# Moving a quad's data in parts: bulk transfers by batch and transposed loads by half tiles in a chunked recurrence kernel

## The chip, the cores and the metric

The kernel runs on one core of a Trainium2 chip. The core has five engines with a queue each: TensorE (PE in the profile; its weight loads are PEld), VectorE (DVE), ScalarE (ACT), GpSimd (POOL) and SyncE (SP). Each runs its own instructions in order and waits on semaphores for the others. Nearly every data transfer of this kernel is issued by SP, one DMA instruction after another, and carried out by 16 DMA engines that all queues share. The metric is the time of one launch on the device in microseconds (us); the lower the better. The time before is the median of three runs.

## What is computed

A recurrence over 768 tokens for 4 batches x 8 heads with a 40 x 40 state per head, and then a layer of two matrix products with h cos(h) between them, over the 3072 tokens:

```python
for t in range(S):                     # S = 768; B, H, D = 4, 8, 40
    y[:, :, t] = einsum('bhd,bhde->bhe', r_t, state)
    Sa = einsum('bhde,bhe->bhd', state, a_t)
    state = state * w_t[:, :, None, :] - einsum('bhd,bhe->bhde', Sa, b_t)
    state = state + einsum('bhd,bhe->bhde', v_t, k_t)
x = y.transpose(0, 2, 1, 3).reshape(B * S, H * D)      # 3072 x 320
h = x @ w_in                                            # 320 x 2048
out = (h * cos(h)) @ w_out                              # 2048 x 320
```

## The kernel before

**Chunks.** The tokens are cut into 24 chunks `c` of 32 tokens, so that 4 batches x 32 tokens fill 128 partitions. Within a chunk the recurrence is turned into small matrix products: `p1` (four segments w, a, b, n) prepares w's products over the chunk and the matrix `nps` whose triangular inverse is needed; `p2` (v, k, g) turns v, k and r and makes the `gram` products; `main` (t, q, x, s, z) carries the state: `ch_t` turns the state (`sT`) and copies it to `s`, `ch_q` reads r, `ch_x` and `ch_s` solve, `ch_z` makes the new state in `qz` and the output `yt`. p1 runs about four chunks ahead, p2 one ahead.

**The layer.** `tokens(c)` stores `yt` to HBM (`xd`, L881) and reads it back as `xT` (L891, L893). For each pair `g` of chunks, 16 "pieces" follow: `first_a`/`first_b` multiply `xT` by w_in (`ph`), ACT and DVE take the cosine (`turns`, L935 to L945), and `second` multiplies by w_out (`po`). The pieces of pair g are allowed from chunk 2g + 2 on; they fill TensorE between the segments of the recurrence.

**The order.** It is written out by hand. For each chunk a list `segs` names segments and places `M` for pieces. `step(work)` runs one segment's Python, which appends its instructions to every engine's queue; then each entry of `waiting` is counted down by one, and what reaches zero is appended. `later(n, work)` puts work there: it stands in the queues n steps later. A step is a position in the queues, not a time.

**Quads.** From chunk 8 on, w, a and r are not turned by TensorE. They come by quads `q` of four chunks, with 32 heads (b, h) x 4 chunks on 128 partitions:

- `ws_fetch(q)` (L164) reads w for a quad into `ws`: one DMA of 128 rows of 5 KB. `ws_scan` makes running products W on DVE. `ws_store` (L247) writes `ws` to HBM (`wd`), from where `load` (L155) reads w in natural order.
- `quad_fetch` (L186) reads a or r into a tile `raw`, one DMA as well. `quad_a` makes a~ = a times the product before it, permuted to d before t (`flip`, L227 on DVE and L232 on ACT), in four slices of d, one a step. `quad_flip` permutes r or W in four copies on ACT (L213, 128 x 320 each).
- `quad_store` writes a `flip` to HBM as `td`: for a~ and W one DMA (L200), whose row order is that of the partitions; for r four (L203), one for each batch, as r's rows are ordered with the head outermost.
- `fetch_T` (L243) reads a chunk of `td` into a transposed tile, in two DMAs, one for each half of the partitions: W into `wb` and a~ into `aT` (`fetch_aw`), r into `rT` (`fetch_r`). `own_w` on POOL (L487, L466) then takes columns of `wb`; POOL's `ch_z` of that chunk reads them.
- `raw` and `flip` share the two buffers of the tag `cv`.

`scanned(q)` is a segment that stands near the end of chunks 4, 8, 12 (for q = 3, 4, 5), within chunk 3 (q = 2), and in the start (q = 1). It scans quad q's w and then schedules, in steps from there: wd's store at 2, a~'s four slices at 1 to 4 and its store at 6, r's fetch (quad q - 1) at 7, its copies at 12 to 15 and its store at 17, W's copies at 18 to 21 and its store at 23, the next quad's w at 25 and a at 26. r of the last quad has a place of its own in chunk 17: fetch at 1, copies at 6 to 9, store at 11.

`p1_w(c)` for c from 8 issues the loads of two chunks of W at once (four DMAs), `p1_a(c)` later those of a~ (four DMAs). `p1_b` calls `own_w` for both chunks at once. `query` issues `fetch_r(c + 2)` one step after `ch_q(c)`.

Of the kernel before, what the change touches and what calls it, by code (L numbers as in the profile page):

```python
# [9 lines left out]
F32 = mybir.dt.float32  # L10
# [10 lines left out]
def kernel(  # L21
# [43 lines left out]
    nc = tc.nc  # L65
    B, H, S, D = r.shape
    P, C, DP = 128, 32, 64
    HH = H // 2
    NCH = S // C
# [89 lines left out]
    ws = const.tile([P, C, D], F32, tag="ws", name="ws")  # L159
    wd = {}  # L160

    def ws_fetch(q, via=nc.sync):
        n = 4 * C * D
        via.dma_start(  # L164
            ws.rearrange("p t d -> p (t d)"),
            bass.AP(w.tensor, w.offset + q * n, [[S * D, B * H], [C * D, 4], [1, C * D]]),
        )

    def ws_scan(q):
        n = 1  # L170
# [9 lines left out]

    td = {}

    def quad_fetch(n, q, via=nc.sync):
        raw = sb2.tile([P, C, D], F32, tag="cv", name="raw")
        x = src[n]
        via.dma_start(  # L186
            raw.rearrange("p t d -> p (t d)"),
            bass.AP(x.tensor, x.offset + q * 4 * C * D, [[S * D, B * H], [C * D, 4], [1, C * D]]),
        )
        G["raw", n] = raw  # L190

    def quad_tile():
        return sb2.tile([P, D, C], F32, tag="cv", name="flip")

    def quad_store(n, q, t, of_heads):
        to = dram.tile([4, H * B, D * C], F32, tag=f"td_{n}", name="td")
        td[n, q] = to
        x = t.rearrange("p d t -> p (d t)")
        if not of_heads:
            nc.sync.dma_start(to.rearrange("c m x -> m c x"), x)  # L200
            return
        for i in range(B):
            nc.sync.dma_start(to.rearrange("c (h b) x -> b h c x", b=B)[i], x[blk[i]])  # L203

    def quad_flip(n, q, raw, of_heads, start):

        t = []

        def part(i):
            if not i:  # L210
                t.append(quad_tile())
            ds = slice(i * D // 4, (i + 1) * D // 4)
            nc.scalar.copy(t[0][:, ds], raw()[:, :, ds].rearrange("p t d -> p d t"))  # L213

        for i in range(4):
            later(start + i, lambda i=i: part(i))
        later(start + 5, lambda: quad_store(n, q, t[0], of_heads))

    def quad_a(q, start):
        t = []  # L220

        def part(i):
            raw = G["raw", "a"]
            if not i:
                t.append(quad_tile())
            ds = slice(i * D // 4, (i + 1) * D // 4)
            nc.vector.tensor_tensor(  # L227
                t[0][:, ds, 1:], raw[:, 1:, ds].rearrange("p t d -> p d t"),
                ws[:, : C - 1, ds].rearrange("p t d -> p d t"), ALU.mult,
            )  # L230
            if i == 3:
                nc.scalar.copy(t[0][:, :, 0:1], raw[:, 0:1].rearrange("p t d -> p d t"))  # L232

        for i in range(4):
            later(start + i, lambda i=i: part(i))
        later(start + 5, lambda: quad_store("a", q, t[0], False))

    def fetch_T(n, c, dst, of_heads):

        x = td[n, c // 4][c % 4].rearrange("m (d t) -> d m t", t=C)  # L240
        for e in range(2):
            at_e = x[:, 4 * B * e : 4 * B * (e + 1)] if of_heads else x[:, e::2]
            nc.sync.dma_start(dst[half[e]].rearrange("p (m t) -> p m t", t=C), at_e)  # L243

    def ws_store(q):
        wd[q] = dram.tile([B, H, 4, C, D], F32, tag="wd", name="wd")
        nc.sync.dma_start(wd[q].rearrange("b h c t d -> (b h c) (t d)"), ws.rearrange("p t d -> p (t d)"))  # L247

    for c in range(2):
        load(c, "w", parts=range(2))  # L250
# [159 lines left out]
    def later(steps, work):  # L410
        waiting.append([steps, work])
# [17 lines left out]
    def p1_w(c):  # L429
        if c >= QT:  # L430
            if c == 8:
                later(2, lambda: over_w(c, unpad(nat["w", c])))
            else:
                over_w(c, unpad(nat["w", c]))
            for i in range(2):
                fetch_aw(c + i, "w")
            return
        ps = at("wT")
        for i in range(2):
            turned(ps[:, i], nat["w", c + i])  # L440
        if c < 4:

            for i in range(2):
                nc.scalar.copy(G["w1"][:, i, :, 0:1], b4(ps[:, i])[:, :, 0:1])
            nc.vector.memset(ps[:, :, ::C], 0.0)
        for i in range(2):
            wb = wb_b[(c + i) % 7]
            if c < 4:
                nc.vector.tensor_tensor_scan(
                    wb[:, 1:], ps[:, i], flat(G["w1"][:, i]), 0.0, ALU.mult, ALU.add  # L450
                )
            else:
                nc.scalar.copy(wb[:, 1:], ps[:, i])
            wc = ring.tile([P, 4 * B], F32, tag="wc", name="wc")
            nc.gpsimd.tensor_copy(wc, wb[:, C::C])
            G["wb", c + i] = wb
            G["wx", c + i] = wb[:, : 4 * P].rearrange("p (f m b t) -> p f m b t", f=2, m=2, t=C)
            G["wc", c + i] = wc.rearrange("p (f m b) -> p f m b", f=2, m=2)
            if c >= 4:
                from_one(c + i)  # L460
        if c >= 4:
            over_w(c, unpad(nat["w", c]))
# [8 lines left out]
        nc.gpsimd.tensor_tensor(unpad(bn_b[c % 7]), unpad(nat["b", c]), rw, ALU.mult)  # L471
        G["rw", c] = rw

    def fetch_aw(c, n):

        if n == "a":
            G["aT", c] = ring.tile([P, B, 4, C], F32, tag="aT", name="aT")
            fetch_T("a", c, G["aT", c].rearrange("p b j t -> p (b j t)"), False)
            return
        wb = wb_b[c % 7]  # L480
        fetch_T("w", c, wb[:, 1:], False)
        G["wb", c] = wb

    def own_w(c):
        wb = G["wb", c]
# [14 lines left out]
    def p1_a(c):  # L500
        if c >= QT:
            over_w(c + 1, unpad(nat["w", c + 1]))
            for i in range(2):
                fetch_aw(c + i, "a")
            return
        if c >= 4:
            ps = at("aps")
            for i in range(2):
                turned(ps[:, i], nat["a", c + i])
            for i in range(2):  # L510
                a_W(c + i, ps[:, i])
            over_w(c + 1, unpad(nat["w", c + 1]))
            return
        for c in range(c, c + 2):
            wn = ps_h.tile([P, 512], F32, tag="h", name="wn")
            aps = ps_o.tile([P, 512], F32, tag="o", name="aps")
            for j in range(4):
                nc.tensor.transpose(
                    wn[:, j * P : (j + 1) * P], G["wb", c][:, j * P + 1 : (j + 1) * P + 1], ident
                )  # L520
            from_one(c)
            turned(aps, nat["a", c])
            over_w(c, unpad(wn.rearrange("p (h d) -> p h d", h=H)))
            a_W(c, aps)

    def p1_b(c):
        ps = at("bT")
        for i in range(2):
            turned(ps[:, i], bn_b[(c + i) % 7])
        for i in range(2):  # L530
            bT = sb3.tile([P, 4, P], F32, tag="opT", name="bT")
            nc.scalar.copy(bT.rearrange("p j t -> p (j t)"), ps[:, i])
            G["bT", c + i] = bT
            if c >= QT:
                own_w(c + i)
        if c == 2:
            G.pop("lower")()

# [163 lines left out]
            for i, n in enumerate("kvr" if c + 1 < QT else "kv"):  # L702
                later(3 + i if c > 1 else 1, lambda n=n: load(c + 1, n))

    def fetch_r(c):
        G["rT", c] = sb2.tile([P, 4, P], F32, tag="rT", name="rT")
        fetch_T("r", c, G["rT", c].rearrange("p j t -> p (j t)"), True)

    def p2_v(c):
        ps = at("vT")  # L710
# [302 lines left out]
    def scanned(q):  # L1013

        ws_scan(q)
        later(2, lambda: ws_store(q))
        if 4 * q < QT:
            later(12, lambda: ws_fetch(q + 1))
            return
        quad_a(q, 1)  # L1020
        if q > 2:
            later(7, lambda: quad_fetch("r", q - 1))
            quad_flip("r", q - 1, lambda: G["raw", "r"], True, 12)
        quad_flip("w", q, lambda: ws, False, 18)
        if q + 1 < NCH // 4:
            later(25, lambda: ws_fetch(q + 1))
            later(26, lambda: quad_fetch("a", q + 1))

    def p2(c):
        def last():  # L1030
# [6 lines left out]
    def main(c):  # L1037
        def last():
            ch_z(c)
            if c + 2 < NCH:  # L1040
                later(8 if c == 2 else 1, lambda: p2_kn(c + 2))

        def query():
            ch_q(c)
            if QT <= c + 2 < NCH:
                later(1, lambda: fetch_r(c + 2))

        return [lambda: ch_t(c), query, lambda: ch_x(c), lambda: ch_s(c), last]

    with tc.manual_schedule():  # L1050
# [119 lines left out]
        for c in range(NCH):  # L1170
# [51 lines left out]
                segs = [t, v, M, q, M, x, k, M, g, M, s, M, M, z, M, M]  # L1222
            n = len(segs)
            if c == 3:
                later(4, lambda: quad_fetch("a", 2))
            if c == NCH - 7:
                later(1, lambda: quad_fetch("r", NCH // 4 - 1))
                quad_flip("r", NCH // 4 - 1, lambda: G["raw", "r"], True, 6)

            goal = 8 * (c + 1) - (18 if c < 19 else 20)  # L1230
            empty, places = 0, segs.count(M)
# [66 lines left out]
```

## Time and profile before

| | us |
|---|---|
| median of 3 runs | 815.8 (814.25 to 816.31) |
| the profiled execution, its own time | 815.19 |
| its span, first to last instruction | 813.3 |
| mean granted TensorE clock | 0.957 |
| TensorE matmul busy | 746.3 |
| VectorE / ScalarE / GpSimd busy | 480.9 / 396.1 / 193.6 |
| SP waiting for `yt` before xd | 154.9 (22 times) |
| SP waiting for `ot` before the output | 75.8 (12 times) |
| SP waiting for xd before xT | 39.7 (23 times) |
| ACT waiting for r's fetch before a copy | 16.5 (3 times, 9.4 the longest) |
| DMA, mean over the span | 88 GB/s, 71.47 MB |

"Busy" is time in which an engine executes; matmuls are pipelined, so a busy TensorE need not be at its peak. The granted clock is the share of TensorE's full clock that it was given. In the timeline a line gives start, duration, engine, source line, operation, what is written from what, the shape and the number of instructions merged; brackets hold the engine's idle time just before and what released it. For SP the duration is the time to issue the DMA, not to carry it out.

### The profile page before, as it was taken

How to read it: one execution, taken by the hardware profiler on the slowest of the kernel's cores; microseconds unless marked ns; L12 is line 12 of the kernel's file. 1: busy time of each engine (PE TensorE's matmuls, PEld its weight loads, DVE VectorE, ACT ScalarE, POOL GpSimd, SP SyncE). 2: the span in 40 equal slices, each digit the busy share in tenths (PEclk: the TensorE clock that was granted, in tenths of full speed). 3: DMA queues.
4: the chain of work that ended last, by engine and by line, in shares of the span. 5: the costliest groups of instructions: out<-in, count | busy, mean ns of one | idle time of the engine just before them, and what ended most of it. 6: DMA issues, size and time to landing. Idle time of an engine off the chain costs nothing.

```text
span 813.3 us, 39086 instructions
## 1 busy us (share of the span) xinstructions
PE 746.3 (92%) x17620; PEld 564.4 (69%) x17620; DVE 480.9 (59%) x1025; ACT 396.1 (49%) x727; POOL 193.6 (24%) x338
## 2 busy tenths in 40 slices
PE   4668889998997999999999999999999999999997
PEld 4545567676675667777777777677787767777775
DVE  8776757865624598473796654894346863332231
ACT  1336666574336334457335466534644345354352
POOL 5316624220322023221220230232031022201000
PEclk9877899999897999999999999999999999999999
DMA  8675463445446443264444455323440221101000
GB/s 111 157 188 141 130 151 82 89 122 148 85 134 162 88 71 66 56 155 98 145 68 69 97 135 110 74 56 59 90 94 21 46 45 44 28 14 36 19 17 16
DMA packets 213829, 71.47 MB, mean 88 GB/s; under 512 B 185120, under 2 KB 206624, under 8 KB 213664
## 3 DMA queue, kind: packets, MB, share of 16 engines
q1 hardware_dynamic: 207968, 67.84, 37.2%
q8 instruction: 138, 2.26, 1.2%
q10 hardware_dynamic: 5440, 0.82, 0.8%
q0 software_dynamic: 256, 0.33, 0.3%
q14 instruction: 27, 0.22, 0.1%
HBM read 49.94 MB, written 19.01 MB: 85 GB/s over the span
## 4 chain that ended last, share of the span: by engine, by line
PE 63%; DVE 16%; DMA 5%; ACT 5%; issue 4%; POOL 3%; SPq 3%; DVEq 0%; POOLq 0%; ACTq 0%
PE ph L101 23%; PE po L101 18%; PE dps L101 4%; PE x0ps L101 3%; PE gram L101 3%; DVE rw L470 2%; SPq L155 2%; PE sps L101 2%; DVE inv_tmp L595 2%; DVE inv L599 2%; PE qps L101 2%; PE nps L101 1%; PE vT L397 1%; DVE turns L937 1%; ACT turns L942 1%
## 5 line engine op out<-in xcount | busy, mean ns | idle before, releaser
L101 PE MATMUL po<-w_out_sb,gT 128*128 128x320 f32 x768 | 227.0, 444 | 0.0
L101 PE MATMUL ph<-xT,w_in_sb 128*128 128x256 f32 x768 | 189.8, 394 | 3.9 <-issue 3.1
L101 PEld LDWEIGHTS po<-w_out_sb,gT 128*128 128x128 f32 x768 | 142.3, 193 | 56.0 <-issue 4.5
L101 PEld LDWEIGHTS ph<-xT,w_in_sb 128*128 128x128 f32 x768 | 142.9, 194 | 36.2 <-issue 16.8
L937 DVE SCALAR_TENSOR_TENSOR turns<-turns,ph 128x512 f32<-128x512 f32 x96 | 63.6, 683 | 116.9 <-ACT turns L935 116.8
L935 ACT ACTIVATE turns<-ph,rnd 128x512 f32<-128x512 f32 x96 | 64.1, 686 | 139.1 <-PE ph L101 138.6
L862 POOL TENSOR_TENSOR qz<-qz,wc 128x160 f32<-128x160 f32 x92 | 42.0, 472 | 207.1 <-DVE qz L861 206.4
L945 DVE TENSOR_TENSOR gT<-ph,turns 128x512 f32<-128x512 f32 x96 | 65.8, 687 | 40.8 <-ACT turns L942 40.8
L941 ACT ACTIVATE turns<-turns 128x512 f32<-128x512 f32 x96 | 60.2, 627 | 23.8 <-DVE turns L937 23.8
L942 ACT ACTIVATE turns<-turns,half_pi 128x512 f32<-128x512 f32 x96 | 69.3, 722 | 3.1
L101 PE MATMUL ph<-xT,w_in_tail 64*128 64x256 f32 (+1 forms) x512 | 55.1, 395 | 0.0
L599 DVE TENSOR_TENSOR inv<-inv,inv_tmp 128x31 f32<-128x31 f32 (+15 forms) x124 | 50.4, 406 | 4.2
L861 DVE TENSOR_TENSOR qz<-dps,qz 128x160 f32<-128x160 f32 x92 | 29.2, 317 | 38.1 <-PE dps L101 38.0
L595 DVE TENSOR_TENSOR inv_tmp<-u,inv 128x31 f32<-128x31 f32 (+15 forms) x124 | 48.3, 390 | 2.3
L687 POOL COPY vp<-nat_v 128x320 f32<-128x320 f32 x24 | 11.6, 484 | 153.5 <-DMA nat_v<-in_v_dram 108.1
L471 POOL TENSOR_TENSOR bn<-nat_b,rw 128x320 f32<-128x320 f32 x22 | 21.8, 989 | 102.3 <-DVE rw L470 89.6
L470 DVE RECIPROCAL rw<-nat_w 128x320 f32<-128x320 f32 x20 | 42.9, 2142 | 0.0
L765 ACT COPY s<-sT 128x512 f32<-128x512 f32 x46 | 24.5, 585 | 31.7 <-PE sT L761 31.5
L101 PEld LDWEIGHTS ph<-xT,w_in_tail 64*128 64x128 f32 (+1 forms) x512 | 32.7, 160 | 8.7 <-issue 5.3
L872 POOL TENSOR_TENSOR yt<-yt,wb 128x512 f32<-128x512 f32 x24 | 31.6, 1316 | 22.3 <-DVE yt L867 22.3
L777 ACT COPY qz<-qps 40x512 f32<-40x512 f32 x46 | 26.6, 579 | 13.8 <-PE qps L101 13.4
L749 ACT COPY vvm<-gram 128x256 f32<-128x256 f32 x24 | 8.8, 368 | 49.9 <-DVE ag L744 49.4
(141 smaller groups left out, 1070.7 us busy)
## 6 DMA issues: line engine op xcount, KB each, us to landing
td<-flip SPq DMA_DIRECT2D x8, 640.0 KB
words<-in_moe_w_in_dram SPq DMA_DIRECT2D x8, 512.0 KB
xd<-yt SPq DMA_DIRECT2D x48, 80.0 KB
out_dram<-ot SPq DMA_DIRECT2D x24, 160.0 KB
nat_k<-in_k_dram SPq DMA_DIRECT2D x92, 40.0 KB
nat_v<-in_v_dram SPq DMA_DIRECT2D x92, 40.0 KB
ws<-in_w_dram SPq DMA_DIRECT2D x5, 640.0 KB
wd<-ws SPq DMA_DIRECT2D x5, 640.0 KB
```

The lines of the kernel that those rows point to most:

```text
L101: nc.tensor.matmul(o, lhsT=lhsT, rhs=rhs, start=start, stop=stop, skip_group_check=True)
L470: nc.vector.reciprocal(rw, wn)
L595: nc.vector.tensor_tensor(tmp, u[:, j : j + 1, :j].to_broadcast([P, C - j, j]), x[:, j:, j : j + 1].to_broadcast([P, C - j, j]), ALU.mult,)
L599: nc.vector.tensor_tensor(x[:, j:, :j], x[:, j:, :j], tmp, ALU.subtract)
L861: nc.vector.tensor_tensor(z, pick(dp, 0, (2 * N72 + C, 2), (N72, 2), (1, D)), z, ALU.add)
L862: nc.gpsimd.tensor_tensor(z, z, wc[:, :, :, bb].unsqueeze(3).to_broadcast([P, 2, 2, D]), ALU.mult,)
L872: nc.gpsimd.tensor_tensor(yt, yt, wx.rearrange("p f m b t -> p (f m) b t"), ALU.mult)
L935: nc.scalar.activation(n, u, ACTF.Identity, bias=rnd, scale=1.0)
L937: nc.vector.scalar_tensor_tensor(n, n, -ROUND, u, ALU.add, ALU.subtract)
L941: nc.scalar.activation(n, n, ACTF.Abs)
L942: nc.scalar.activation(n, n, ACTF.Sin, bias=half_pi, scale=-2.0 * math.pi)
L945: nc.vector.tensor_tensor(gT[:, 2 * e : 2 * e + 2].rearrange("p f t -> p (f t)"), us[e], ns[e], ALU.mult)
```

## The change

Every bulk transfer of a quad is cut into four DMAs, one for each batch i (32 partitions), and `spread` puts them a step apart. The source of a fetch is then written as 8 heads x 4 chunks x 5 KB instead of 32 x 4 x 5 KB. The stores of a~ and W are written by batch too; r's store was so already. The two halves of a transposed load become separate steps: after `p1_w(c)` eight steps hold one DMA each, first the four of a~, then the four of W, and `p1_a` issues none. `own_w` comes eight steps after `p1_b`. The steps of `scanned(q)` from q = 2 on become: wd's store at 2 to 5, a~'s at 6 to 9, r's fetch at 5 to 8, its copies at 12 to 15 as before, its store at 16 to 19, W's copies at 16 to 19 and its store at 20 to 23, the next w at 23 to 26, the next a at 28 to 31. r of the last quad takes the same steps (fetch at 5 to 8, copies from 12). In chunk 3 the fetch of a goes from step 4 to steps 3 to 6. In the start the four parts of w's fetch stand directly behind one another, and so do those of its store.

On PE and DVE the order of the instructions does not change. On ACT W's copies move two steps forward (in the quads fetched at chunks 5, 9 and 13), and r's last four move back. On POOL the small operations of `own_w` move back. SP's queue gets 78 more DMAs.

```diff
+    def in_quads(x, q, i):
         n = 4 * C * D
-        via.dma_start(
-            ws.rearrange("p t d -> p (t d)"),
-            bass.AP(w.tensor, w.offset + q * n, [[S * D, B * H], [C * D, 4], [1, C * D]]),
+        return bass.AP(
+            x.tensor, x.offset + q * n + i * H * S * D, [[S * D, H], [C * D, 4], [1, C * D]]
         )
+
+    def ws_fetch(q, via=nc.sync, parts=range(B)):
+        for i in parts:
+            via.dma_start(ws[blk[i]].rearrange("p t d -> p (t d)"), in_quads(w, q, i))
...
+    def spread(start, work):
+        for i in range(B):
+            later(start + i, lambda i=i: work(i))
+
+    def quad_fetch(n, q, start):
+        def part(i):
+            if not i:
+                G["raw", n] = sb2.tile([P, C, D], F32, tag="cv", name="raw")
+            nc.sync.dma_start(
+                G["raw", n][blk[i]].rearrange("p t d -> p (t d)"), in_quads(src[n], q, i)
+            )
+        spread(start, part)
...
-    def quad_store(n, q, t, of_heads):
...
+    def quad_store(n, q, t, of_heads, i):
+        if not i:
+            td[n, q] = dram.tile([4, H * B, D * C], F32, tag=f"td_{n}", name="td")
+        to, x = td[n, q], t[0][blk[i]].rearrange("p d t -> p (d t)")
+        if of_heads:
+            nc.sync.dma_start(to.rearrange("c (h b) x -> b h c x", b=B)[i], x)
+        else:
+            nc.sync.dma_start(to.rearrange("c (b h) x -> b h c x", b=B)[i], x)
...
-        later(start + 5, lambda: quad_store(n, q, t[0], of_heads))
+        spread(start, part)
+        spread(start + 4, lambda i: quad_store(n, q, t, of_heads, i))
...
-        later(start + 5, lambda: quad_store("a", q, t[0], False))
+        spread(start, part)
+        spread(start + 5, lambda i: quad_store("a", q, t, False, i))
...
+    def fetch_T(n, c, dst, of_heads, e):
         x = td[n, c // 4][c % 4].rearrange("m (d t) -> d m t", t=C)
-        for e in range(2):
-            at_e = x[:, 4 * B * e : 4 * B * (e + 1)] if of_heads else x[:, e::2]
-            nc.sync.dma_start(dst[half[e]].rearrange("p (m t) -> p m t", t=C), at_e)
+        at_e = x[:, 4 * B * e : 4 * B * (e + 1)] if of_heads else x[:, e::2]
+        nc.sync.dma_start(dst[half[e]].rearrange("p (m t) -> p m t", t=C), at_e)
+
+    def ws_store(q, parts=range(B)):
...
+            nc.sync.dma_start(
+                wd[q][i].rearrange("h c t d -> (h c) (t d)"), ws[blk[i]].rearrange("p t d -> p (t d)")
+            )
...
-            for i in range(2):
-                fetch_aw(c + i, "w")
+            for m in range(8):
+                later(1 + m, lambda m=m: fetch_aw(c + m // 2 % 2, "aw"[m // 4], m % 2))
...
-            for i in range(2):
-                fetch_aw(c + i, "a")
...
-                own_w(c + i)
+                later(8, lambda i=i: own_w(c + i))
...
-                later(1, lambda: fetch_r(c + 2))
+                for e in range(2):
+                    later(1 + e, lambda e=e: fetch_r(c + 2, e))
...
         ws_scan(q)
-        later(2, lambda: ws_store(q))
         if 4 * q < QT:
+            later(2, lambda: ws_store(q))
             later(12, lambda: ws_fetch(q + 1))
             return
         quad_a(q, 1)
+        spread(2, lambda i: ws_store(q, [i]))
         if q > 2:
-            later(7, lambda: quad_fetch("r", q - 1))
-            quad_flip("r", q - 1, lambda: G["raw", "r"], True, 12)
-        quad_flip("w", q, lambda: ws, False, 18)
+            quad_r(q - 1)
+        quad_flip("w", q, lambda: ws, False, 16)
         if q + 1 < NCH // 4:
-            later(25, lambda: ws_fetch(q + 1))
-            later(26, lambda: quad_fetch("a", q + 1))
+            spread(23, lambda i: ws_fetch(q + 1, parts=[i]))
+            quad_fetch("a", q + 1, 28)
+
+    def quad_r(q):
+        quad_fetch("r", q, 5)
+        quad_flip("r", q, lambda: G["raw", "r"], True, 12)
...
             if c == 3:
-                later(4, lambda: quad_fetch("a", 2))
+                quad_fetch("a", 2, 3)
             if c == NCH - 7:
-                later(1, lambda: quad_fetch("r", NCH // 4 - 1))
-                quad_flip("r", NCH // 4 - 1, lambda: G["raw", "r"], True, 6)
+                quad_r(NCH // 4 - 1)
```

More of the change, by code (lines that the diff above doesn't have):

```diff
@@ L160 @@
     wd = {}
-    def ws_fetch(q, via=nc.sync):
+    def in_quads(x, q, i):
         n = 4 * C * D
-        via.dma_start(
-            ws.rearrange("p t d -> p (t d)"),
-            bass.AP(w.tensor, w.offset + q * n, [[S * D, B * H], [C * D, 4], [1, C * D]]),
-        )
+        return bass.AP(
+            x.tensor, x.offset + q * n + i * H * S * D, [[S * D, H], [C * D, 4], [1, C * D]]
+        )
+    def ws_fetch(q, via=nc.sync, parts=range(B)):
+        for i in parts:
+            via.dma_start(ws[blk[i]].rearrange("p t d -> p (t d)"), in_quads(w, q, i))
     def ws_scan(q):
@@ L181 @@
     td = {}
[L183 to L190, printed above, removed]
+    def spread(start, work):
[9 more added lines that the diff above has]
+        spread(start, part)
     def quad_tile():
         return sb2.tile([P, D, C], F32, tag="cv", name="flip")
-    def quad_store(n, q, t, of_heads):
[L196 to L203, printed above, removed]
+    def quad_store(n, q, t, of_heads, i):
[6 more added lines that the diff above has]
+            nc.sync.dma_start(to.rearrange("c (b h) x -> b h c x", b=B)[i], x)
     def quad_flip(n, q, raw, of_heads, start):
@@ L213, in part @@
             nc.scalar.copy(t[0][:, ds], raw()[:, :, ds].rearrange("p t d -> p d t"))
-        for i in range(4):
-            later(start + i, lambda i=i: part(i))
-        later(start + 5, lambda: quad_store(n, q, t[0], of_heads))
+        spread(start, part)
+        spread(start + 4, lambda i: quad_store(n, q, t, of_heads, i))
     def quad_a(q, start):
@@ L232, in part @@
                 nc.scalar.copy(t[0][:, :, 0:1], raw[:, 0:1].rearrange("p t d -> p d t"))
-        for i in range(4):
-            later(start + i, lambda i=i: part(i))
-        later(start + 5, lambda: quad_store("a", q, t[0], False))
-    def fetch_T(n, c, dst, of_heads):
+        spread(start, part)
+        spread(start + 5, lambda i: quad_store("a", q, t, False, i))
+    def fetch_T(n, c, dst, of_heads, e):
         x = td[n, c // 4][c % 4].rearrange("m (d t) -> d m t", t=C)
-        for e in range(2):
-            at_e = x[:, 4 * B * e : 4 * B * (e + 1)] if of_heads else x[:, e::2]
-            nc.sync.dma_start(dst[half[e]].rearrange("p (m t) -> p m t", t=C), at_e)
-    def ws_store(q):
-        wd[q] = dram.tile([B, H, 4, C, D], F32, tag="wd", name="wd")
-        nc.sync.dma_start(wd[q].rearrange("b h c t d -> (b h c) (t d)"), ws.rearrange("p t d -> p (t d)"))
+        at_e = x[:, 4 * B * e : 4 * B * (e + 1)] if of_heads else x[:, e::2]
+        nc.sync.dma_start(dst[half[e]].rearrange("p (m t) -> p m t", t=C), at_e)
+    def ws_store(q, parts=range(B)):
+        if 0 in parts:
+            wd[q] = dram.tile([B, H, 4, C, D], F32, tag="wd", name="wd")
+        for i in parts:
+            nc.sync.dma_start(
+                wd[q][i].rearrange("h c t d -> (h c) (t d)"), ws[blk[i]].rearrange("p t d -> p (t d)")
+            )
     for c in range(2):
@@ L472, in over_w, with fetch_aw @@
         G["rw", c] = rw
-    def fetch_aw(c, n):
+    def fetch_aw(c, n, e):
         if n == "a":
-            G["aT", c] = ring.tile([P, B, 4, C], F32, tag="aT", name="aT")
-            fetch_T("a", c, G["aT", c].rearrange("p b j t -> p (b j t)"), False)
+            if not e:
+                G["aT", c] = ring.tile([P, B, 4, C], F32, tag="aT", name="aT")
+            fetch_T("a", c, G["aT", c].rearrange("p b j t -> p (b j t)"), False, e)
             return
-        wb = wb_b[c % 7]
-        fetch_T("w", c, wb[:, 1:], False)
-        G["wb", c] = wb
+        wb = G["wb", c] = wb_b[c % 7]
+        fetch_T("w", c, wb[:, 1:], False, e)
     def own_w(c):
@@ L703, in landed, with fetch_r @@
                 later(3 + i if c > 1 else 1, lambda n=n: load(c + 1, n))
-    def fetch_r(c):
-        G["rT", c] = sb2.tile([P, 4, P], F32, tag="rT", name="rT")
-        fetch_T("r", c, G["rT", c].rearrange("p j t -> p (j t)"), True)
+    def fetch_r(c, e):
+        if not e:
+            G["rT", c] = sb2.tile([P, 4, P], F32, tag="rT", name="rT")
+        fetch_T("r", c, G["rT", c].rearrange("p j t -> p (j t)"), True, e)
     def p2_v(c):
```

## The prediction

> **What bounds the kernel now.** I read the page first: the share of each engine, the forty slices and the chain that ended last.
>
> ```profile
> span 813.3 us, 39086 instructions
> PE 746.3 (92%) x17620; PEld 564.4 (69%) x17620; DVE 480.9 (59%) x1025; ACT 396.1 (49%) x727; POOL 193.6 (24%) x338
> ...
> PE   4668889998997999999999999999999999999997
> ...
> PEclk9877899999897999999999999999999999999999
> ...
> PE 63%; DVE 16%; DMA 5%; ACT 5%; issue 4%; POOL 3%; SPq 3%; DVEq 0%; POOLq 0%; ACTq 0%
> ```
>
> TensorE (PE) is busy for 92% of the span, so 67 us of it are idle, and most of those lie ahead of the eighth slice, in the start. After it one slice stands out: the thirteenth, 244 to 264 us, with PE at 7 and a granted clock of 7. No other later place can give much back, and any new hole in PE lengthens the span. Stretches of ten us show it closer (columns: PE, PEld, DVE, ACT, POOL busy, granted clock, share of the DMA engines, GB/s):
>
> ```profile
> 230.00:240.00 10.00, 9.73 (x229) 7.45 (x228) 2.15 (x10) 0.99 (x2) 4.21 (x7) 1.00 0.54 165
> 240.00:250.00 10.00, 5.73 (x148) 4.57 (x147) 5.74 (x9) 9.75 (x16) 0.87 (x1) 0.77 0.22 75
> 250.00:260.00 10.00, 9.11 (x139) 6.75 (x138) 2.65 (x2) 4.09 (x9) 3.34 (x9) 0.72 0.77 164
> ```
>
> ScalarE (ACT) does nearly nothing for ten us, then is full for ten; PE idles 4.3 us in the second. The timeline of ACT, SP's queue and PE in that place (start, duration; in brackets the idle time before and what ended it):
>
> ```profile
> 223.02 0.40 SPq L247 DMA_DIRECT2D wd<-ws  x1
> 223.52 2.41 SPq L155 DMA_DIRECT2D nat_r<-in_r_dram  x4
> 225.97 5.92 SPq L155 DMA_DIRECT2D nat_b<-in_b_dram  x8
> 232.00 0.57 SPq L200 DMA_DIRECT2D td<-flip  x1
> 232.61 0.60 SPq L186 DMA_DIRECT2D raw<-in_r_dram  x1
> ...
> 239.01 2.24 ACT L213 COPY flip<-raw 128x320 f32<-128x320 f32 x3 [9.38 <-DMA raw<-in_r_dram]
> ...
> 244.70 3.06 SPq L203 DMA_DIRECT2D td<-flip  x4
> ...
> 247.69 0.89 PE L101 MATMUL gram<-rT,vT 40*32 40x32 f32 x64 [3.52 <-ACT rT L718]
> 247.88 0.40 SPq L891 DMA_DIRECT2D xT<-xd  x1
> ```
>
> SP issues without a pause from 207.1 to 233.2 us, so r's fetch goes out only at 232.6 and lands at 239.0. ACT works in order and stands before r's permutation for 9.4 us; vT and rT are copied late, PE waits 3.5 us before `gram`, and xT, queued behind r's stores, makes the next `ph` wait. This is the place that the change has to mend.
>
> **The parts and their prices.** *More issues.* 26 transfers (ws 5, wd 5, raw 8, td of a~ and W 8) become 104: 78 more. A quarter of r's store takes SP 656 ns (median of 16, L203) and a whole store 592 (8, L200), so a part costs as much as the whole: 78 x 0.656 = 51 us of SP's time. What hides it is SP's own waiting: 154.9 us before xd, 75.8 before the output, 39.7 before xT. There is no cover where SP is issuing back to back: 207 to 233 us, 172 to 205, and some 343 to 362.
>
> *Shape.* Each part of a fetch has 8 rows outermost on the DRAM side, as r's store has now, and so have the new stores of a~ and W; only wd keeps 32. Two stretches of 2 us compare whole transfers with that shape:
>
> ```profile
> 234.00:236.00 2.00, 2.00 (x14) 1.52 (x11) 1.58 (x8) 0.00 (x0) 1.79 (x5) 1.00 0.99 312
> 246.20:248.20 2.00, 0.52 (x51) 0.52 (x54) 2.00 (x2) 2.00 (x4) 0.00 (x0) 0.50 0.47 181
> ```
>
> The first is a~'s store and r's fetch, whole: 0.99 of the engines, 312 GB/s. The second is r's store by batch: 0.47 and 181. For 2 x 655 KB = 1.31 MB that is 4.2 against 7.2 us, 3.0 us more where both stand on the path. A row of a fetch in this shape doesn't exist; I take the store's, as the nearest, and nothing (312 GB/s) as the other end.
>
> The Trainium skill, "DMA: Bandwidth & Descriptors", section "Why a DMA increments its semaphore by 16 and not by 1", says that a transfer runs on the largest number of engines up to 16 that divides the slowest dimension of both sides, and on the lowest-numbered ones. By it the 8-row parts run on 8 engines, which agrees with 0.47 here, and it extends this to the fetches: an argument against the change. If it didn't hold for fetches the sum below would lose about 1.8 us.
>
> *Around 240 us.* From xd at 207.1 to the last part of r, SP gets three more parts each of wd (0.40) and raw (0.60) and two of td (0.59) and loses one half-tile load (four of a~ out, three of W in; 0.57): 1.2 + 1.8 + 1.2 - 0.6 = 3.6 us by issue. By the engines: the first part leaves at about 232.6, and the pair needs 7.2 us and the 2.7 us that lie now between 4.2 us of transfer and the 6.9 from 232.0 to 238.9: landed at 242.5, also 3.5 late. The two run side by side, so I take 3 (0 if r comes as now, 5 if the bulk ahead of 207 delays xd too). Nothing brings r forward: the same nat loads stand ahead of it. Then ACT: in the new order two more of W's copies (0.82 each, L213) stand ahead of vT and rT, 1.6 us. `gram` starts 4.6 late. xd now stands behind the first part of r's store, which waits for r's four copies (244.7 + 3), so: store 0.7, xd 0.7, and 2.3 until xT may go (xd 286.55, xT 288.83 in a quiet place): xT at 251.4, landed 3.35 later as in the chain, 254.8. PE after `gram` and `sT` comes to `ph` at 247.69 + 4.6 + 0.8 + 2.0 = 255.1; it was 251.4. **+3.7 us** (0 to 7).
>
> *Chunk 4, 176 us.* Ahead of chunk 3's xd (166.42) stand three more wd and three more td parts: 3 x 0.40 + 3 x 0.59 = 3.0 us. xT waited 4.5 us for xd there, with the bulk in flight; sent after the bulk it should need 1.0 + 2.3, so xT goes at 172.7 instead of 171.9, and the halved rate adds something. `ph` at 175.66 has no slack over it: **+1** (0 to 2.5).
>
> *Quads 3 and 4 (around 365 and 480 us).* r lands 0 to 3 us later by the same rates, and ACT already waits 2.7 and 4.4 us there; two more copies of W stand ahead of the copy of s (+1.6), which idles 1.2 before it. PE has pieces to run: **+1.5 for both** (0 to 4). If the pieces didn't cover, it would be 3 each.
>
> *The start.* b's load for chunk 3 leaves behind three more parts of ws (0.68 each), 2.0 us later; bn at 27.06 stands before it and the whole inversion behind bn. The words' fetch, which competes with it, also moves back: **+0.5** (0 to 2).
>
> *At nothing:* own_w eight steps later on POOL (busy 24%; it was waiting 1.0 us for W there, and ch_z, the reader, is three chunks off); a~ before W (`nps`, its reader, comes after the next chunk's pb); ws and a fetched up to five steps later (their scan is some 100 us away); r of the last quad, whose ACT wait is none today, as rT is read three chunks on. The last part of r leaves at step 8 and the permutation stays at 12, 4 steps instead of 5: only for the last quad does it move back.
>
> *Gain.* Three times after 200 us PE stands in the middle of a run of matmuls with nothing that the profile shows: 1.64 us at 203.2, 1.24 at 261.8, 1.87 at 277.5, the first two beside bulk at full engine share. Thinner bulk may free up to 4.8 us; I take **-1**.
>
> Sum: 3.7 + 1 + 1.5 + 0.5 - 1 = **+5.7 us**. The profiled execution took 815.2 (span 813.3, 1.9 around it), 0.6 below the median of 815.8; so 820.9 there and **821.5** on the median's scale.
>
> **The rivals.** *A, bulk gives way (faster).* If the small fetches pass between the parts, the three holes close (-4.8) and r is hardly late at 240 (+1): 815.8 - 3.8 = 812. It decides if the holes are bulk's doing. For it: the first two stand in or right behind bulk. Against: the third has little DMA beside it (0.24 of the engines from 270 to 290), and the same bytes move. 0.19.
>
> *B, hidden.* SP's waits before xd (8 to 11 us in most chunks) swallow the issues, and the parts overlap as the whole did; 240 costs 1, the gain 1: 816. For it: PE is at 9 and over from 340 us on. Against: no cover at 207 to 233. 0.14.
>
> *C, xT late in each quad.* xd and xT stand behind parts of a store that waits for ACT, at chunks 5, 9 and 13; if the pieces there wait too, 3 us more each at 9 and 13, and 3 of lower clock after a longer hole at 240 (0.72 to 0.83 for 30 us now): 821.5 + 9 = 830. Against: in quads 3 and 4 r's copies end before xd today. 0.14.
>
> **How the numbers follow.** The forecast has 0.53, and the time is its own, 821.5; alone it spans 817.5 to 827. All terms at their upper ends without a gain: 7 + 2.5 + 4 + 2 = 15.5, 831; all at the lower with the whole gain: 811. Both rivals C and A lie inside, so the range is 811 to 831. Over 0.3% (2.4 us), about what a measurement of this kernel tells from no change: slower has the forecast and C, 0.67; same has B, 0.14; faster has A, 0.19.
>
> **What would show it.** Fetches by parts at about half the engine share of 312 GB/s; ACT's wait before r's copies over 9.4 us at 240 and about the same later; `gram` waiting on rT for 6 to 8 us; xd issued after r's first store part; the slice at 244 to 264 no better than 7. It is wrong if r lands before 239, if the wait on rT shrinks, or if the three holes are gone; a loss spread evenly over the span would speak against my place.

## The result and the profile after

The changed kernel takes 828.8 us (median of 4 runs, 827.0 to 831.3) against 816.05 of the kernel before (4 runs, 814.25 to 820.18): a ratio of 1.015, 95% interval 1.010 to 1.020. That is 12.8 us more, slower as forecast and inside the range of 811 to 831, but more than twice the forecast's 5.7 us and past the 817.5 to 827 that the forecast alone spanned. The profiled execution took 827.9 us, its span is 826.0.

The page of the changed kernel, the same rows as before:

```profile
span 826.0 us, 39179 instructions
PE 739.8 (90%) x17620; PEld 561.0 (68%) x17620; DVE 481.4 (58%) x1025; ACT 394.9 (48%) x727; POOL 194.7 (24%) x338
...
PE   4767889899864999998999997999999999999997
...
PEclk8678899999995999999999999999999999999999
...
PE 50%; DVE 16%; SPq 11%; ACT 7%; DMA 7%; issue 4%; POOL 3%; DVEq 0%; ACTq 0%; POOLq 0%
```

PE is busy for 6.5 us less and the span is 12.7 longer, so PE idles 19 us more. The slices show the largest hole: the twelfth and thirteenth stand at 6 and 4 (9 and 7 before). In the chain SP's queue went from 3% to 11% and the DMAs from 5% to 7%. The stretches of ten us (columns as before):

```profile
230.00:240.00 10.00, 9.85 (x174) 7.19 (x169) 1.80 (x8) 0.00 (x0) 4.22 (x7) 1.00 0.61 116
240.00:250.00 10.00, 0.00 (x0) 0.00 (x0) 0.00 (x0) 0.42 (x1) 0.00 (x0) 0.73 0.42 139
250.00:260.00 10.00, 1.10 (x92) 0.97 (x97) 4.78 (x6) 9.73 (x16) 0.00 (x0) 0.50 0.15 52
260.00:270.00 10.00, 10.00 (x184) 8.10 (x175) 3.68 (x5) 4.70 (x9) 3.55 (x6) 0.75 0.56 159
```

From 240 to 250 us no computing engine does anything but the first 0.4 us of one copy. Chunk 4's xd in the kernel before, for comparison:

```profile
207.09 0.74 SPq L881 DMA_DIRECT2D xd<-yt  x2
```

The timelines of SP's queue, ACT and PE in the changed kernel there:

```profile
212.24 0.69 SPq L890 DMA_DIRECT2D xd<-yt  x2
...
239.34 0.75 SPq L196 DMA_DIRECT2D raw<-in_r_dram  x1
240.13 0.70 SPq L212 DMA_DIRECT2D td<-flip  x1
...
243.72 0.68 SPq L196 DMA_DIRECT2D raw<-in_r_dram  x1
244.44 0.64 SPq L212 DMA_DIRECT2D td<-flip  x1
...
249.58 2.23 ACT L222 COPY flip<-raw 128x320 f32<-128x320 f32 x3 [22.62 <-DMA td<-flip]
...
253.96 0.90 PE L101 MATMUL gram<-aT,kT 40*32 40x32 f32 x64 [14.12 <-DVE rt L676]
259.79 0.89 PE L101 MATMUL gram<-rT,vT 40*32 40x32 f32 x64 [4.93 <-ACT rT L727]
```

r's copies need two things: the last part of r in `raw`, and the `flip` buffer, which is the one that a~ leaves (the tag `cv` has two) and which is free only when the last part of a~'s store has landed. These two leave SP last, at 243.7 and 244.4 us, where the whole transfers left at 232.6 and 232.0. The copies start at 249.6 instead of 239.0. ACT works in order, so the `turns` of two pieces behind the copies stand too, DVE stands behind those, and PE waits 14.1 us for DVE's `rt` and then 4.9 for rT.

The same copies at the next two quads, first in the kernel before (quad 3, quad 4):

```profile
361.74 2.97 ACT L213 COPY flip<-raw 128x320 f32<-128x320 f32 x4 [2.67 <-DMA raw<-in_r_dram]
...
477.19 2.95 ACT L213 COPY flip<-raw 128x320 f32<-128x320 f32 x4 [4.44 <-DMA raw<-in_r_dram]
```

Then in the changed kernel, and PE after them (first two lines: quad 3; last two: quad 4):

```profile
374.53 2.94 ACT L222 COPY flip<-raw 128x320 f32<-128x320 f32 x4 [9.65 <-DMA wb<-td]
382.33 1.97 PE L101 MATMUL ph<-xT,w_in_sb 128*128 128x256 f32 x8 [2.36 <-DVE gT L954]
...
492.88 2.96 ACT L222 COPY flip<-raw 128x320 f32<-128x320 f32 x4 [10.84 <-DMA wb<-td]
500.69 3.59 PE L101 MATMUL ph<-xT,w_in_sb 128*128 128x256 f32 x8 [4.23 <-DVE gT L954]
```

ACT waited 2.7 and 4.4 us there before, and PE did not wait for `gT`. (The copies do not read wb; its load stands right behind the pair in SP's queue.)

To see where the 13 us come in, I set ACT's 349 activations, whose order is the same in both kernels, side by side, start after minus start before:

| at (before, us) | 134 | 183 | 222 | 281 | 340 | 396 | 454 | 509 | 800 |
|---|---|---|---|---|---|---|---|---|---|
| changed kernel, us late | 0.4 | 1.6 | -1.7 | 5.6 | 6.4 | 9.5 | 9.3 | 15.6 | 13.1 |

Three stairs, +7.3 at 240, +3.1 between 340 and 396, +6.3 between 454 and 509, and some 6 us of gains before, between and behind them. Each stair is a place where r's copies stand.

### The profile page after: what moved, and what is told of

The parts are those of the page before. It is cut to its first block, busy times and chain, and to the rows that moved or that the text cites. A ratio compares the mean times of both kernels' runs of the same rounds, so it can differ in the third digit from the quotient of the medians.

```text
span 826.0 us, 39179 instructions
## 1 busy us (share of the span) xinstructions
PE 739.8 (90%) x17620; PEld 561.0 (68%) x17620; DVE 481.4 (58%) x1025; ACT 394.9 (48%) x727; POOL 194.7 (24%) x338
## 4 chain that ended last, share of the span: by engine, by line
PE 50%; DVE 16%; SPq 11%; ACT 7%; DMA 7%; issue 4%; POOL 3%; DVEq 0%; ACTq 0%; POOLq 0%
PE ph L101 20%; PE po L101 13%; SPq L155 6%; PE x0ps L101 3%; DVE inv_tmp L603 3%; DVE rw L480 3%; DVE inv L607 2%; PE dps L101 2%; PE gram L101 2%; PE sps L101 2%; DVE turns L946 2%; ACT flip L222 2%; PE qps L101 1%; ACT turns L951 1%; DMA ws<-in_w_dram 1%
## 5 line engine op out<-in xcount | busy, mean ns | idle before, releaser
L101 PE MATMUL po<-w_out_sb,gT 128*128 128x320 f32 x768 | 223.2, 439 | 0.0
L101 PEld LDWEIGHTS po<-w_out_sb,gT 128*128 128x128 f32 x768 | 140.2, 190 | 54.3 <-issue 1.7
L786 ACT COPY qz<-qps 40x512 f32<-40x512 f32 x46 | 26.6, 578 | 15.5 <-PE qps L101 15.1
L222 ACT COPY flip<-raw 128x320 f32<-128x320 f32 x16 | 12.0, 807 | 44.6 <-DMA td<-flip 22.6
```

The source lines that it names most:

```text
L101: nc.tensor.matmul(o, lhsT=lhsT, rhs=rhs, start=start, stop=stop, skip_group_check=True)
```

## The experiments

Each ratio is against the kernel before in the same series of runs, whose median was 812.7 to 815.4 us.

**1. Bulk in parts alone.** The loads as they were:

```diff
-            for m in range(8):
-                later(1 + m, lambda m=m: fetch_aw(c + m // 2 % 2, "aw"[m // 4], m % 2))
+            for i in range(2):
+                for e in range(2):
+                    fetch_aw(c + i, "w", e)
...
-                later(8, lambda i=i: own_w(c + i))
+                own_w(c + i)
```

> The changed kernel with the half-tile loads of a~, W and r, and own_w, back where they were before; the bulk stays in four parts, the copies stay where the change put them. Theory (the bulk's parts end late and ScalarE stands before r's copies): nearly the whole loss stays, 824 to 830 us, with ScalarE's wait before r's copies near 240 us at 15 us or more (22.6 in the changed kernel, 9.4 before). Rival (the loads, a~ sent first at 204 us, make chunk 4's xd 5 us late and everything behind it): 815 to 820 us, and xd of chunk 4 back near 207 us.

Measured: 828.3 us, ratio 1.017 (1.012 to 1.023), ACT's wait near 240 us 22.1. xd of chunk 4 still left at 212.8. The whole loss is in the bulk; it is the bulk, not the order of the loads, that makes SP late at chunk 4.

**2. The loads alone.** The kernel before with the loads of the change:

```diff
-            for i in range(2):
-                fetch_aw(c + i, "w")
+            for m in range(8):
+                later(1 + m, lambda m=m: fetch_aw(c + m // 2 % 2, "aw"[m // 4], m % 2))
...
-                own_w(c + i)
+                later(8, lambda i=i: own_w(c + i))
```

> The kernel before with only the half-tile loads moved as in the change (a~ first, a half tile a step, own_w eight steps later, r's two halves a step apart); bulk whole. Theory: 814 to 819 us, ScalarE's wait near 240 us at 9 to 12 us. Rival (the loads' order does it): 823 us or more, with xd of chunk 4 at 210 us or later and r's fetch pushed behind it.

Measured: 812.35 us, 0.999 (0.995 to 1.003); ACT waits 9.0 us near 240 and xd leaves at 207.6. The loads by half tiles and `own_w` eight steps later neither cost nor bring time that shows.

**3. As many parts, another shape.** Each part of a fetch, and of a~'s and W's stores, takes a quarter of the columns of all rows:

```diff
-            x.tensor, x.offset + q * n + i * H * S * D, [[S * D, H], [C * D, 4], [1, C * D]]
+            x.tensor, x.offset + q * n + i * C // 4 * D,
+            [[S * D, B * H], [C * D, 4], [1, C // 4 * D]],
...
-            nc.sync.dma_start(to.rearrange("c (b h) x -> b h c x", b=B)[i], x)
+            nc.sync.dma_start(td[n, q].rearrange("c m x -> m c x")[:, :, xs], x)
```

> The changed kernel, but each part of a fetch and of a store of a~ and W takes a quarter of the columns of all 32 rows instead of all columns of 8 rows: as many issues, the same bytes, the same order. If the eight outermost rows (half the DMA engines) make the parts late: more than 10 packets of a fetch at once (up to 18), r and a~ landed about 2 us after their last issue instead of 5, and 817 to 823 us. If the issues and steps alone make them late: 825 to 831 us.

Measured: 814.5 us, 1.001 (0.998 to 1.004), less than the 817 to 823 expected. With the same issues in the same order nearly the whole loss is gone from the time. The groups of r's copies, changed kernel first, then this one (busy and mean, then the idle time before them and what ended it):

```profile
L222 ACT COPY flip<-raw 128x320 f32<-128x320 f32 x16 | 12.0, 807 | 44.6 <-DMA td<-flip 22.6 <-DMA wb<-td 20.5 <-DMA raw<-in_r_dram 1.5
```

```profile
L226 ACT COPY flip<-raw 128x320 f32<-128x320 f32 x16 | 12.0, 808 | 33.9 <-DMA td<-flip 20.8 <-DMA wb<-td 13.0
```

The wait at quads 3 and 4 falls from 20.5 to 13.0 us together; the one near 240 only from 22.6 to 20.8. In the packets of the trace, the 1.31 MB of r's fetch and a~'s store at quad 3 took 5.9 us whole (up to 19 packets at once), 12.7 in parts of 8 rows (up to 10) and 9.3 in parts by columns (up to 20). The shape shows at SP too. The second and third part of a~'s store at quad 3, changed kernel first:

```profile
363.61 2.14 SPq L212 DMA_DIRECT2D td<-flip  x1
...
367.61 1.47 SPq L212 DMA_DIRECT2D td<-flip  x1
```

```profile
362.19 0.79 SPq L216 DMA_DIRECT2D td<-flip  x1
...
364.77 0.81 SPq L216 DMA_DIRECT2D td<-flip  x1
```

An issue of 0.8 us takes up to 2.1 with parts of 8 rows. From the first issue of the pair to the end of its last, loads between them included, SP takes 11.5 and 13.0 us at quads 3 and 4 in the changed kernel, 8.8 and 10.6 here, and 3.9 and 4.6 in the kernel before. So the shape shows in the issues; how it makes an issue longer was not tried. At 240 us what stays is lateness of issue: xd leaves at 212.2 as in the changed kernel, and the pair last at 243.6 and 244.2. Set beside the kernel before as in the table above, this kernel is 1.9 us ahead at 222 us and 5.0 late at 281, then 5.4 at 340, 5.2 at 509 and 1.2 at 800. The two later stairs are gone and the one near 240 is not; gains elsewhere make up for it.

**4. r's copies later.** The transfers of the change, r's and W's copies four steps later and the next fetch of w two (`quad_r` takes the copies' first step, 12 in the change, as an argument):

```diff
-            quad_r(q - 1)
-        quad_flip("w", q, lambda: ws, False, 16)
+            quad_r(q - 1, 16)
+        quad_flip("w", q, lambda: ws, False, 20)
```

> The changed kernel with r's copies four steps later (16 instead of 12), W's copies behind them (20 instead of 16) and the next fetch of W two steps later; the transfers of r and a~ stay. If ScalarE, standing in order before r's copies, is what turns late parts into lost time: its waits before r's copies fall (22.6, 9.7 and 10.8 us in the changed kernel) and the time is 812 to 821 us. If the late data itself is what counts (r's or W's tiles too late for their readers, xT behind the stores): 826 us or more, with new waits for r's or W's tiles.

Measured: 817.5 us, 1.006 (1.003 to 1.009). More than half of the loss goes with the bulk as late as ever: ACT's place in the order turns late parts into lost time. Near 240 us four steps are not enough. ACT still waits 14.8 us before the first copy, and PE 14.6 for rT, whose copy stands behind three of r's:

```profile
256.31 0.89 PE L101 MATMUL gram<-rT,vT 40*32 40x32 f32 x64 [14.60 <-ACT rT L727]
```

**5. The pair whole.** The changed kernel with only r's fetch and a~'s store in one transfer each:

```diff
-    def quad_fetch(n, q, start):
+    def quad_fetch(n, q, start, whole=False):
...
+            later(start + 2, all_rows)
+            return
         spread(start, part)
...
-        spread(start + 5, lambda i: quad_store("a", q, t, False, i))
...
+        later(start + 5, store)
...
-        quad_fetch("r", q, 5)
+        quad_fetch("r", q, 5, True)
```

> The changed kernel with only r's fetch and a~'s store whole again (one transfer each, at the steps they had before); W's fetch and stores, a~'s fetch and r's store stay in parts. If this pair, on which ScalarE's copies of r wait, carries the loss at 370 and 490 us: the waits there fall from 9.7 and 10.8 us to 2 to 6 and the time is 814 to 820 us; near 240 us some 5 us stay, since SP still comes to chunk 4's xd at 212 us instead of 207. If the other parts carry it: 824 us or more.

Measured: 815.2 us, 1.001 (0.998 to 1.004). The waits at quads 3 and 4 are 2.2 and 2.9 us, and no PE wait for `gT` is left there. Near 240 us ACT still waits 18.8: xd of chunk 4 leaves at 212.3 and the pair at 239.7 and 240.3. The group of r's copies:

```profile
L233 ACT COPY flip<-raw 128x320 f32<-128x320 f32 x16 | 12.0, 808 | 23.9 <-DMA raw<-in_r_dram 23.9
```

Beside the kernel before it is 2.1 us ahead at 222 us, 2.1 late at 281 and 1.6 ahead at 800: the loss near 240 is there, and gains elsewhere hide it.

**6. Only the pair in parts.** The kernel before, with that pair alone in four parts of 8 rows:

```diff
-        later(start + 5, lambda: quad_store("a", q, t[0], False))
+        for i in range(4):
+            later(start + 5 + i, lambda i=i: a_part(q, t, i))
...
-            later(7, lambda: quad_fetch("r", q - 1))
+            for i in range(4):
+                later(5 + i, lambda i=i: r_part(q - 1, i))
```

> The kernel before with only that pair in four parts of 8 rows, a step apart (the last quad's fetch left whole); all else as before. If the pair carries the loss: 819 to 828 us against about 813, ScalarE's waits before r's copies at 12 us or more near 240 and 6 us or more at 365 and 480; xd of chunk 4 stays at 207 us. If it takes the other parts' issues on SP as well: 812 to 817 us.

Measured: 822.0 us, 1.010 (1.006 to 1.014), the waits 14.0, 9.8 and 7.8 us, and xd at 206.3. The group of r's copies:

```profile
L228 ACT COPY flip<-raw 128x320 f32<-128x320 f32 x16 | 12.1, 810 | 31.5 <-DMA td<-flip 17.5 <-DMA xd<-yt 14.0
```

So the pair alone carries about two thirds of the change's loss (1.0 of 1.5%, with an interval of 0.6 to 1.4). With experiments 1 and 5 the likely rest is the other parts' issues ahead of the pair: with them xd leaves at 212 us, without them at 206.

**7. The kernel before, copies later.**

```diff
-            quad_flip("r", q - 1, lambda: G["raw", "r"], True, 12)
-        quad_flip("w", q, lambda: ws, False, 18)
+            quad_flip("r", q - 1, lambda: G["raw", "r"], True, 16)
+        quad_flip("w", q, lambda: ws, False, 20)
```

> The kernel before with r's copies four steps later and W's two, transfers as they were. If ScalarE's standing in order (9.4 us near 240, 2.7 and 4.4 later) costs TensorE time already here: 806 to 811 us against about 813, and the slice at 244 to 264 us better than 7. If not, 811 to 816 us; if the later tiles of r or W are what their readers then wait for, more.

Measured: 806.9 us (804.3 to 808.8), 0.989 (0.986 to 0.992), faster than both kernels. The wait of r's copies:

```profile
L213 ACT COPY flip<-raw 128x320 f32<-128x320 f32 x16 | 12.6, 808 | 4.5 <-DMA raw<-in_r_dram 4.5
```

It was 16.5. Two stretches of this kernel show the place after 240 us:

```profile
240.00:250.00 10.00, 6.10 (x147) 5.03 (x146) 5.66 (x5) 9.05 (x15) 1.07 (x2) 0.83 0.43 106
250.00:260.00 10.00, 10.00 (x276) 7.92 (x275) 2.71 (x5) 7.80 (x15) 3.03 (x9) 1.00 0.74 187
```

PE has 10.0 us and the whole clock from 250 to 260, where the kernel before has 9.11 and 0.72.

**8. W's copies back at 18.** The changed kernel with one number undone:

```diff
-        quad_flip("w", q, lambda: ws, False, 16)
+        quad_flip("w", q, lambda: ws, False, 18)
```

> The changed kernel with W's four copies back at step 18 (the change has them at 16). By the prediction two copies of 0.82 us come out from ahead of vT and rT near 240 us, and of s at 375 and 490 us: 2 to 5 us less than the changed kernel, 823 to 827 us. If ScalarE's two copies lie beside other work: 827 to 830 us.

Measured: 827.3 us, 1.016 (1.009 to 1.023), not told from the change. The interval is wider than the 2 to 5 us looked for, so the time does not decide. The profile does, near 240 us:

```profile
250.74 2.23 ACT L222 COPY flip<-raw 128x320 f32<-128x320 f32 x3 [24.16 <-DMA td<-flip]
...
259.40 0.90 PE L101 MATMUL gram<-rT,vT 40*32 40x32 f32 x64 [3.38 <-ACT rT L727]
```

From r's first copy to `gram` with rT it takes 8.7 us here and in the kernel before (239.01 to 247.69), 10.2 in the changed kernel (249.58 to 259.79). So the two copies are worth 1.5 us of that way; in this profile the copies start 1.2 us later, which covers most of it.

**9 to 11. Both menders, and more steps.** Parts by columns with the copies at 16 and 20; the pair whole with the copies at 16 and 20; the kernel before with the copies at 18 and 22:

```diff
-            quad_flip("r", q - 1, lambda: G["raw", "r"], True, 12)
-        quad_flip("w", q, lambda: ws, False, 18)
+            quad_flip("r", q - 1, lambda: G["raw", "r"], True, 18)
+        quad_flip("w", q, lambda: ws, False, 22)
```

> The changed kernel with both menders at once: parts by columns of all 32 rows, and r's copies at step 16, W's at 20. If these two are the whole loss and the parts bring nothing by themselves: 806 to 812 us, the ratio to the kernel before equal to that of the kernel before with later copies (0.989). If parts also help (smaller pieces let small loads through): under 804 us. If the 78 extra issues cost on their own: 812 to 816 us.

> The changed kernel with the pair whole, and r's copies at step 16, W's at 20; all other transfers in parts of 8 rows. By the theory that only the pair and the place of the copies count: 806 to 812 us, as the run with parts by columns. If the other parts of 8 rows cost time of their own: 3 us or more above it.

> The kernel before with r's copies six steps later (18) and W's four (22), transfers as they were. With four steps ScalarE still waited 4.1 us near 240 and gram 3.9 us for rT behind three of r's copies. If these go: 803 to 807 us. If the stores of r and W then come too late for their readers: 808 us or more.

Measured: 807.2 us, 0.992 (0.987 to 0.996); 807.8, 0.992 (0.990 to 0.995); 808.2, 0.994 (0.991 to 0.997). All three are faster than the kernel before, and none is told from experiment 7. Mended, the parts neither cost nor bring time that shows. That is a sum: near 240 us PE still waits 11.5 and 11.6 us for rT in the first two, against 3.9 in experiment 7, and they make it up elsewhere. In the third both waits are gone as expected (ACT has no idle time before r's copies, PE none before `gram` with rT), and the time is still not under 808: two more steps bring nothing further, and why is open.

## Why the prediction was right, and where not

*The place and the chain* (bulk late, ACT before r's copies, PE behind it) held near 240 us. But the two later quads, where I had ACT's wait "about the same", cost more together (9.4 us) than that place (7.3). Parts in flight run at half the engine share (0.50 and 125 GB/s from 239 to 245 us, against 0.99 and 312), xd leaves after r's first store part (256.0 after 255.3), and the slice at 244 to 264 us is worse than 7. The rule cited from the Trainium skill, "DMA: Bandwidth & Descriptors", section "Why a DMA increments its semaphore by 16 and not by 1", was borne out for fetches: fetches with no store near them had up to 10 packets at once with 8 rows outermost, up to 21 with all rows. What the shape costs in time is experiment 3 against the change, 1.015 to 1.001.

*The range* held by luck in part. The three stairs, 16.7 us, are more than all my terms at their upper ends (15.5), and two terms left their own ranges. The time lies under 831 since some 6 us came back, of which I had forecast 1.

*Around 240 us, +3.7 (0 to 7).* Measured +7.3. The step that failed is "r lands 3 late": the copies start 10.6 late. Chunk 4's xd was 5.15 us late already, which I had named as the upper bound and not taken. From there to r's last part SP took 31.5 us instead of 25.5 (I had 3.6 more): the parts of r and a~ alternate at 0.7 us each, and xT now waits 3.4 us for xd with fewer loads between. And I had let the later issue (3.6) and the slower transfer (3.5) run side by side, where they add up: the first of the pair leaves 7.3 us late (239.3 against 232.0), and from there to the copies it takes 10.2 us against 7.0. `gram` waits for rT 4.9 us, not 6 to 8; the larger wait, 14.1, stands ahead of it, since the pieces' `turns` are queued behind r's copies. I had named the copies of vT and rT as what is behind and left those out.

*W's two copies, 1.6 us near 240 and again at the later quads.* Near 240 they are there, 1.5 us by experiment 8's profile, though its time does not show them. At the later quads I had them ahead of the copy of s, but PE waits there for `gT`; what they cost there is not shown.

*Quads 3 and 4, +1.5 together (0 to 4).* Measured 3.1 and 6.3. This is the term that was furthest too small. I let r land "0 to 3 us later by the same rates" and let PE's pieces cover it. ACT's waits grew by 7.0 and 6.4 us. It is not the rate at which the last part lands: from the end of the pair's last issue to the copies it takes 3.5 and 3.2 us, no more than before (3.7 and 5.2). It is SP's issues, 11.5 and 13.0 us for the pair instead of 3.9 and 4.6, which I had not priced there. Rival C had put 3 us more on each and came nearest in size (830), but by another way: xd and xT behind r's store. In experiments 4, 7, 9 and 10 it is the place of the copies that decides, and in the changed kernel PE waits there for `gT`, not for xT. (In experiment 4 it does wait for xT at these quads, 1.3 and 1.8 us.)

*Chunk 4, +1.* Between 134 and 183 us the changed kernel loses 1.2, but then regains 3.3 by 222. The start's +0.5 stands at 0.4 by 134 us. It rises to 2 to 3 us in between, and does so as well in experiment 2, which leaves the start's transfers alone, so no cause is shown.

*The holes, -1.* Too little. PE's idle times of over 0.8 us with no releaser, after 100 us, come to 10.8 us before and 3.9 after; between 190 and 300 us to 4.8 and 0. I had named the three holes' being gone as a sign that I was wrong, and they are gone. This is rival A's premise, and it holds in the other profiles: 10.8 to 17.9 us in the five profiles in which the bulk other than the pair is whole (before, experiments 2, 6, 7, 11), 2.9 to 5.7 in the eight in which it is in parts. So A was right about the holes and wrong about the time, as the three stairs, 16.7 us together, take more than twice as much back. What of a whole transfer goes with PE's stops was not tried.

*B* fell with the pair and near 240 us. In the sum the other parts cost nothing that shows (experiment 5, 1.001), but SP's waits do not hide their issues at 240, where xd leaves 5 us late; gains elsewhere cover that. The issues of the pair, for which r's copies wait, are not hidden (experiment 6, 1.010).

## What to carry to other kernels

When a transfer is cut, look at the outermost dimension of each part: for 1.31 MB at quad 3, parts of 8 rows had up to 10 packets in flight and took 12.7 us, parts of all rows up to 20 and 9.3 us, the whole up to 19 and 5.9 us. Then ask what waits for the last part, on which in-order engine, and what stands behind it there: the same late data cost 1.5% with the copies at one place and 0.6% with them four steps later. A reader that an engine meets before its data is worth moving first: here it brought 1.1% in the kernel before without touching a transfer.

## What the runs showed of the hardware that was not expected

SP's issue of one 160 KB part of a~'s store took 0.64 us at 244.4 us and 2.77 at quad 4 (481.35 us), both behind other 8-row parts. Long issues are not theirs alone: one transposed load took 3.4 us in the changed kernel (207.18 us) and 3.4 in the kernel before (350.07 us), where the bulk is whole. TensorE's granted clock was 0.50 from 250 to 260 us, behind ten us of an idle PE, and 0.75 in the next ten. Eight matmuls of `ph` took 3.2 us at 262.4 and 2.0 at 268.0, so a hole costs more than its length. And the kernels that move most of their bulk in whole 655 KB transfers have some 7 us more of short PE stops that no wait explains than those with parts of 164 KB, of either shape; the cause is open.
